# Lightning attention with a highway layer on one core: plain f32 loads with casts on Pool, and the feed-forward computed transposed in groups of four chunks

## The chip, the cores and the metric

The kernel runs on one core of a Trainium2 chip. The metric is device time in microseconds (us) for one execution; lower is better. TensorE is called PE, VectorE DVE, ScalarE ACT, GpSimd POOL (Pool), SyncE SP. Pool issues software DMAs, which can change the type on the way; SP and ACT issue hardware DMAs, which copy as is. PSUM is the memory that PE writes, SBUF the memory that DMA writes.

## What is computed

q, k and v have 4 batches, 8 heads, 768 positions and 64 features, all in f32. Positions go in blocks, and a state carries what came before:

```python
intra = einsum(qb, kb) * Dmask;  intra = einsum(intra, vb)   # Dmask = lam**(i-j) for i >= j
inter = einsum(qb * lam_pow, kv_state)
out   = intra + inter
kv_state = lam_block * kv_state + einsum(kb * rev_pow, vb)
# the heads side by side: x has 3072 rows and 512 columns
H = maximum(x @ w_h, 0);  T = sigmoid(x @ w_t + b_t)
y = T * H + (1 - T) * x                                      # 3072 x 512, f32
```

The kernels take blocks of 128 positions, which is the same sum cut otherwise, and put the powers of lam into v (pow_k) and into the attention's output (pow_q), so that the state itself needs no decay.

## The kernel before, in words

A chunk n is 128 positions of one batch with all 8 heads; there are 6 chunks a batch and N = 24 in all. The order of the work is written out by hand: the program calls helpers, and each engine runs its instructions in the order of these calls.

- Loads. k (one DMA per chunk, L58) and q (one per head, L53) are issued by Pool and cast to bf16 on the way. v comes as f32 on SP's queue (L64 for a whole batch, L67 for chunks of batch 0). The weights wh, wt are cast loads on Pool (L98, L99). The lam loads stand first on SP's queue (L71 to L75). Two buffers per batch tile (`load`), so a batch's loads are issued when the batch two before it ends (L262 to L266).
- `scale_v` (L165, Pool) multiplies a chunk of v by pow_k into bf16 vs. `trans_k` (L158 on PE, L160 on ACT) turns k, `trans_q` (L150, L151) turns a pair of heads of q for a whole batch, in the four turns before it is used. Both go through the one PSUM tile tr.
- `scores` (L173) makes s_ps from kT and qT, and DVE masks it (L176). `attn` adds the state's part (inter, L184) and the masked part (intra, L188) in o_ps; DVE multiplies by pow_q into xT (L191), features on partitions. `state` (L200) adds to kv_ps, and ACT copies it into s_bd (L204).
- The feed-forward of one chunk: `ffn_xh` turns xT back by matmuls with the identity (L209, copied by ACT to x_sb, L211) and computes x @ w_h with xT as the weights and wh moving (L214); DVE makes hmx = max(h, 0) - x (L216). `ffn_t` does x @ w_t (L221), adds the bias by one more matmul (L222: a row of ones times the bias, split in two bf16 rows prepared on DVE at L126 to L134), and ACT takes the sigmoid (L224). `combine` multiplies on DVE (thmx, L228), adds x on Pool (o_sb, L230), and SP stores (L231).
- A turn i of the loop (L245) runs ffn_xh(i-1), scores(i+1), scale_v(i+1), attn(i), state(i), trans_q, ffn_t(i-1), combine(i-1), trans_k(i+2). All PSUM tiles have one buffer.

Of the kernel before, what the change touches and what calls it, by code (L numbers as in the profile page):

```python
# [16 lines left out]
def kernel(  # L17
# [21 lines left out]
    N = B * NCH  # L39

# [7 lines left out]
    qb, kb, vf = {}, {}, {}  # L48

    def load_q(b):  # L50
        qb[b] = load.tile([QP, J, H, D], BF16, tag="qb", name=f"qb{b}")
        for h in range(H):
            nc.gpsimd.dma_start(out=qb[b][:, :, h, :], in_=q[b, h].rearrange("(p j) d -> p j d", j=J))  # L53

    def load_k(b, c):
        if b not in kb:
            kb[b] = load.tile([C, NCH, H, D], BF16, tag="kb", name=f"kb{b}")
        nc.gpsimd.dma_start(out=kb[b][:, c], in_=k[b, :, c * C:(c + 1) * C, :].rearrange("h p d -> p h d"))  # L58

    def load_v(b, cs=None):  # L60
        if b not in vf:
            vf[b] = load.tile([C, H, NCH, D], F32, tag="vf", name=f"vf{b}")
        if cs is None:
            nc.sync.dma_start(out=vf[b].rearrange("p h c d -> p (h c) d"),  # L64
                              in_=v[b].rearrange("h (c p) d -> p (h c) d", p=C))
        else:
            nc.sync.dma_start(out=vf[b][:, :, cs, :],  # L67
                              in_=v[b, :, cs * C:(cs + 1) * C, :].rearrange("h p d -> p h d"))

    lam_bc = singles.tile([128, H], F32)  # L70
    nc.sync.dma_start(out=lam_bc, in_=lam.partition_broadcast(128))  # L71
    lam_hp = singles.tile([128, NP], F32)
    lam_v = lam.rearrange("(p two) -> two p", two=2)
    nc.sync.dma_start(out=lam_hp[0:64, :], in_=lam_v[0].partition_broadcast(64))
    nc.sync.dma_start(out=lam_hp[64:128, :], in_=lam_v[1].partition_broadcast(64))  # L75
    load_k(0, 0)
    load_q(0)
    load_v(0, 0)
    load_v(0, 1)
    bt_f = singles.tile([128, DM], F32)  # L80
    nc.sync.dma_start(out=bt_f[0:1, :], in_=moe_b_t.partition_broadcast(1))
    nc.sync.dma_start(out=bt_f[32:33, :], in_=moe_b_t.partition_broadcast(1))
# [15 lines left out]
    nc.gpsimd.dma_start(out=wh, in_=moe_w_h.rearrange("(kc p) n -> p kc n", p=128))  # L98
    nc.gpsimd.dma_start(out=wt, in_=moe_w_t.rearrange("(kc p) n -> p kc n", p=128))  # L99
    for c in range(2, NCH):  # L100
        load_k(0, c)
        load_v(0, c)
    load_q(1)
    for c in range(NCH):
        load_k(1, c)
    load_v(1)
# [8 lines left out]
    nc.vector.tensor_copy(tq_f, tq_i)  # L115
    pk_ln = singles.tile([128, H, NCH], F32)
# [8 lines left out]
    ones_r = singles.tile([128, 128], BF16)  # L125
    nc.vector.memset(ones_r, 0.0)  # L126
    nc.vector.memset(ones_r[0:1, :], 1.0)
    nc.vector.memset(ones_r[32:33, :], 1.0)
    bt = singles.tile([128, DM], BF16)
    nc.vector.memset(bt, 0.0)  # L130
    bt_h = singles.tile([128, DM], BF16)
    nc.vector.tensor_copy(bt[0:1, :], bt_f[0:1, :])
    nc.vector.tensor_copy(bt_h[32:33, :], bt_f[32:33, :])
    nc.vector.tensor_tensor(bt[32:33, :], in0=bt_f[32:33, :], in1=bt_h[32:33, :], op=ALU.subtract)  # L134

    s_bd = []
    for i in range(2):
        t = singles.tile([128, NP, 128], BF16, name=f"s_bd{i}")
        nc.vector.memset(t, 0.0)
        s_bd.append(t)  # L140


    qT, kT, vs, masked, xT, x_sb, hps, tps, t_sb, hmx, kv_ps, o_ps = ({} for _ in range(12))

    def trans_q(b, hp):
        if hp == 0:
            qT[b] = load.tile([128, NP, NCH, J * PP], BF16, tag="qT", name=f"qT{b}")
        tr = ps.tile([128, J, QP], BF16, tag="tr", name="tr")
        for j in range(J):
            nc.tensor.transpose(tr[:, j, :], qb[b][:, j, 2 * hp:2 * hp + 2, :], id128[0:QP, 0:QP])  # L150
        nc.scalar.activation(qT[b][:, hp].rearrange("p c (q j) -> p (c q) j", j=J),  # L151
                             tr.rearrange("p j q -> p q j"), AF.Copy)

    def trans_k(n):
        b, c = divmod(n, NCH)
        tr = ps.tile([128, NP, C], BF16, tag="tr", name="tr")
        for hp in range(NP):
            nc.tensor.transpose(tr[:, hp, :], kb[b][:, c, 2 * hp:2 * hp + 2, :], id128)  # L158
        kT[n] = work.tile([128, NP, C], BF16, tag="kT", name="kT")
        nc.scalar.activation(kT[n], tr, AF.Copy)  # L160

    def scale_v(n):
        b, c = divmod(n, NCH)
        vs[n] = work.tile([C, H, D], BF16, tag="vs", name="vs", bufs=3)
        nc.gpsimd.tensor_tensor(vs[n], in0=vf[b][:, :, c, :], in1=pow_k[:, :, c, :].to_broadcast([C, H, D]), op=ALU.mult)  # L165
# [13 lines left out]
    def attn(n):  # L179
        b, c = divmod(n, NCH)  # L180
        o_ps[n] = ps.tile([128, NP, C], F32, tag="o", name="o_ps")
        for hp in range(NP):
            if c > 0:
                nc.tensor.matmul(o_ps[n][:, hp, :], lhsT=s_bd[n % 2][:, hp, :], rhs=qT[b][:, hp, c, :],  # L184
                                 start=(hp == 0), stop=False, skip_group_check=True)
        for hp in range(NP):
            for e in range(2):
                nc.tensor.matmul(o_ps[n][64 * e:64 * e + 64, hp, :], lhsT=vs[n][:, 2 * hp + e, :], rhs=masked[n][:, e, hp, :],  # L188
                                 start=(hp == 0 and c == 0), stop=True, skip_group_check=True)
        xT[n] = work.tile([128, NP, C], BF16, tag="xT", name="xT")  # L190
        nc.vector.tensor_tensor(xT[n], in0=o_ps[n], in1=pow_q[:, :, c * C:(c + 1) * C], op=ALU.mult)  # L191

    def state(n):
# [5 lines left out]
        for hp in range(NP):  # L199
            nc.tensor.matmul(kv_ps[b][:, hp, :], lhsT=kb[b][:, c, 2 * hp:2 * hp + 2, :], rhs=vs[n][:, 2 * hp:2 * hp + 2, :],  # L200
                             start=(c == 0 and hp == 0), stop=True, skip_group_check=True)
# [4 lines left out]
    def ffn_xh(n):  # L206
        x_ps = ps.tile([C, DM], F32, tag="x", name="x_ps")
        for kc in range(KC):
            nc.tensor.matmul(x_ps[:, kc * 128:(kc + 1) * 128], lhsT=xT[n][:, kc, :], rhs=id128, start=True, stop=True)  # L209
        x_sb[n] = work.tile([C, DM], BF16, tag="x_sb", name="x_sb", bufs=3)  # L210
        nc.scalar.activation(x_sb[n], x_ps, AF.Copy)  # L211
        h_ps = ps.tile([C, DM], F32, tag="h", name="h_ps")
        for kc in range(KC):
            nc.tensor.matmul(h_ps, lhsT=xT[n][:, kc, :], rhs=wh[:, kc, :], start=(kc == 0), stop=(kc == KC - 1))  # L214
        hmx[n] = work.tile([C, DM], BF16, tag="hmx", name="hmx")
        nc.vector.scalar_tensor_tensor(hmx[n], in0=h_ps, scalar=0.0, in1=x_sb[n], op0=ALU.max, op1=ALU.subtract)  # L216

    def ffn_t(n):
        t_ps = ps.tile([C, DM], F32, tag="t", name="t_ps")
        for kc in range(KC):  # L220
            nc.tensor.matmul(t_ps, lhsT=xT[n][:, kc, :], rhs=wt[:, kc, :], start=(kc == 0), stop=False)  # L221
        nc.tensor.matmul(t_ps, lhsT=ones_r, rhs=bt, start=False, stop=True)  # L222
        t_sb[n] = work.tile([C, DM], BF16, tag="t_sb", name="t_sb")
        nc.scalar.activation(t_sb[n], t_ps, AF.Sigmoid)  # L224

    def combine(n):
        thmx = work.tile([C, DM], BF16, tag="thmx", name="thmx")
        D_ENG.tensor_tensor(thmx, in0=t_sb[n], in1=hmx[n], op=ALU.mult)  # L228
        o_sb = work.tile([C, DM], F32, tag="o_sb", name="o_sb", bufs=3)
        nc.gpsimd.tensor_tensor(o_sb, in0=thmx, in1=x_sb[n], op=ALU.add)  # L230
        nc.sync.dma_start(out=out[n * C:(n + 1) * C, :], in_=o_sb)  # L231

    D_ENG = nc.vector

    scale_v(0)
    trans_k(0)
    for hp in range(NP):
        trans_q(0, hp)
    scores(0)
    for hp in range(NP):  # L240
        nc.scalar.activation(pow_q[:, hp, C:], tq_f[:, C:], AF.Exp, scale=ln_hp[:, hp:hp + 1])
    trans_k(1)

# [53 lines left out]
```

## Time and profile before

| | us |
|---|---|
| median of 3 runs | 197.85 (196.64 to 197.92) |
| the profiled execution, its own time | 197.84 |
| its span, first to last instruction | 196.0 |
| PE busy in the span | 105.8 |
| Pool busy | 101.8 |
| ACT busy | 74.7 |
| DVE busy | 74.3 |

The mean granted PE clock was 0.912 of full. HBM gave 20.98 MB and took 6.29 MB.

How to read the rows shown further on. A row of groups has line, engine, operation, output <- inputs, shapes, count, then busy us, mean ns of one, and the idle time before these instructions with what ended most of it. A row of the timeline has the start in us, the length, engine, line, operation, shapes and count. A row of waits has who waited for whom, the total in us, how often, and the longest. A row of windows has the stretch in us, its length, each engine's busy time with its instructions in brackets, the granted PE clock, the mean number of busy queue shares of the DMA engines, and GB/s written. Ends of matmuls are modelled, so starts are the safer reading.

### The profile page before, as it was taken

What the parts mean: (1) busy time and instruction counts of PE and PEld (TensorE: products, weight loads), DVE (VectorE), ACT (ScalarE), POOL (GpSimd) and SP (SyncE); (2) the same over time, 40 slices, a digit from 0 to 9 for tenths busy, and PEclk for the clock granted to TensorE, in tenths of its full rate; (3) what the DMA queues carried; (4) which work ended last, traced back from release to release, by engine and by line L of the source; (5) the groups of instructions that cost most, each with busy time, mean ns of one, the idle gap of its engine ahead of it and who ended that gap; (6) DMA issues with size and microseconds to landing.
All of it is one profiled execution on the core that took longest, in us unless ns stands there. A gap on an engine that the chain in (4) does not pass through costs nothing.

```text
span 196.0 us, 2858 instructions
## 1 busy us (share of the span) xinstructions
PE 105.8 (54%) x1080; PEld 61.0 (31%) x1080; DVE 74.3 (38%) x132; ACT 74.7 (38%) x142; POOL 101.8 (52%) x116
## 2 busy tenths in 40 slices
PE   0013420000797999000499999100299999999980
PEld 0012310000454555000255554000155555455440
DVE  0044040000155667300046666400036666677640
ACT  3045450000557663100147764100047765556630
POOL 7585531189304456943644445961835444655442
PEclk9999999999999999955589999955579999999999
DMA  0899999999501111999931111799962211112112
GB/s 5 69 170 171 187 182 228 185 129 141 37 0 53 55 55 57 182 209 159 140 64 54 57 53 53 142 214 168 141 34 80 82 55 53 57 55 110 53 53 107
DMA packets 66160, 20.10 MB, mean 103 GB/s; under 512 B 57442, under 2 KB 63074, under 8 KB 66148
## 3 DMA queue, kind: packets, MB, share of 16 engines
q0 software_dynamic: 51104, 7.34, 59.7%
q1 hardware_dynamic: 15044, 12.60, 26.0%
q8 instruction: 8, 0.13, 0.3%
q14 instruction: 4, 0.03, 0.1%
HBM read 20.98 MB, written 6.29 MB: 139 GB/s over the span
## 4 chain that ended last, share of the span: by engine, by line
issue 41%; DMA 30%; POOL 27%; POOLq 1%
DMA kb<-in_k_dram 24%; POOL vs L165 13%; DMA qb<-in_q_dram 6%; POOL qb L53 6%; POOL o_sb L230 4%; POOL kb L58 4%; POOLq L292 1%; POOLq L165 0%; POOLq L230 0%; POOLq L58 0%; POOLq L281 0%
## 5 line engine op out<-in xcount | busy, mean ns | idle before, releaser
L230 POOL TENSOR_TENSOR o_sb<-thmx,x_sb 128x512 f32<-128x512 bf16 x24 | 27.7, 1153 | 57.9 <-DVE thmx L228 57.9
L53 POOL DMA_DIRECT2D qb<-in_q_dram x32 | 24.7, 775 | 29.2 <-DMA kb<-in_k_dram 21.9
L176 DVE TENSOR_TENSOR masked<-s_ps,tri 128x512 bf16<-128x512 f32 x48 | 30.7, 681 | 9.7 <-PE s_ps L173 9.7
L204 ACT ACTIVATE s_bd<-kv_ps 64x256 bf16<-64x256 f32 x40 | 15.1, 378 | 49.8 <-PE kv_ps L200 49.4
L150 PE MATMUL tr<-id,qb 96*128 96x96 bf16 x128 | 10.2, 237 | 42.9 <-DMA qb<-in_q_dram 38.6
L228 DVE TENSOR_TENSOR thmx<-t_sb,hmx 128x512 bf16<-128x512 bf16 x24 | 10.2, 425 | 56.9 <-issue 51.2
L151 ACT ACTIVATE qT<-tr 128x768 bf16<-128x768 bf16 x16 | 13.0, 811 | 40.5 <-PE tr L150 40.3
L221 PE MATMUL t_ps<-wt,xT 128*128 128x512 bf16 x96 | 26.5, 400 | 0.0
L214 PE MATMUL h_ps<-wh,xT 128*128 128x512 bf16 x96 | 25.7, 392 | 0.0
L165 POOL TENSOR_TENSOR vs<-vf,pow_k 128x512 bf16<-128x512 f32 x24 | 25.4, 1068 | 0.0
L191 DVE TENSOR_TENSOR xT<-o_ps,pow_q 128x512 bf16<-128x512 f32 x24 | 16.4, 682 | 20.1 <-PE o_ps L188 20.1
L58 POOL DMA_DIRECT2D kb<-in_k_dram x24 | 21.7, 926 | 3.3 <-DMA qb<-in_q_dram 2.5
L216 DVE SCALAR_TENSOR_TENSOR hmx<-h_ps,x_sb 128x512 bf16<-128x512 f32 x24 | 16.6, 692 | 17.9 <-ACT x_sb L211 9.3
L150 PEld LDWEIGHTS <-qb 96*128 96x128 bf16 x128 | 8.2, 115 | 43.8 <-DMA qb<-in_q_dram 37.8
L188 PE MATMUL o_ps<-masked,vs 128*64 128x128 bf16 x192 | 10.3, 231 | 20.7 <-POOL vs L165 20.7
L224 ACT ACTIVATE t_sb<-t_ps 128x512 bf16<-128x512 f32 x24 | 14.3, 595 | 14.0 <-PE t_ps L222 14.0
L158 PE MATMUL tr<-id,kb 128*128 128x128 bf16 x96 | 10.3, 236 | 16.3 <-POOL id masks.py:199 11.8
L158 PEld LDWEIGHTS <-kb 128*128 128x128 bf16 x96 | 8.0, 106 | 23.6 <-DMA kb<-in_k_dram 10.9
L160 ACT ACTIVATE kT<-tr 128x512 bf16<-128x512 bf16 x24 | 14.2, 592 | 1.1 <-PE tr L158 0.7
L211 ACT ACTIVATE x_sb<-x_ps 128x512 bf16<-128x512 f32 x24 | 14.3, 597 | 0.1
L188 PEld LDWEIGHTS <-vs 128*64 128x64 bf16 x192 | 6.3, 113 | 23.4 <-POOL vs L165 21.0
L173 PE MATMUL s_ps<-qT,kT 64*128 64x128 bf16 x192 | 10.4, 229 | 3.3 <-ACT kT L160 2.9
(42 smaller groups left out, 94.0 us busy)
## 6 DMA issues: line engine op xcount, KB each, us to landing
out_dram<-o_sb SPq DMA_DIRECT2D x24, 256.0 KB, 2.0
kb<-in_k_dram POOLq DMA_DIRECT2D x24, 128.0 KB, 12.0
qb<-in_q_dram POOLq DMA_DIRECT2D x32, 96.0 KB, 10.5
vf<-in_v_dram SPq DMA_DIRECT2D x6, 256.0 KB, 10.8
wh<-in_moe_w_h_dram POOLq DMA_DIRECT2D x1, 512.0 KB, 14.0
wt<-in_moe_w_t_dram POOLq DMA_DIRECT2D x1, 512.0 KB, 17.1
vf<-in_v_dram SPq DMA_DIRECT2D x3, 0.2 KB, 12.2
lam_hp<-in_lam_dram SPq DMA_DIRECT2D x2, 1.0 KB, 7.4
```

Source lines behind the costliest of these rows:

```text
L53: nc.gpsimd.dma_start(out=qb[b][:, :, h, :], in_=q[b, h].rearrange("(p j) d -> p j d", j=J))
L58: nc.gpsimd.dma_start(out=kb[b][:, c], in_=k[b, :, c * C:(c + 1) * C, :].rearrange("h p d -> p h d"))
L150: nc.tensor.transpose(tr[:, j, :], qb[b][:, j, 2 * hp:2 * hp + 2, :], id128[0:QP, 0:QP])
L158: nc.tensor.transpose(tr[:, hp, :], kb[b][:, c, 2 * hp:2 * hp + 2, :], id128)
L165: nc.gpsimd.tensor_tensor(vs[n], in0=vf[b][:, :, c, :], in1=pow_k[:, :, c, :].to_broadcast([C, H, D]), op=ALU.mult)
L176: nc.vector.tensor_tensor(masked[n][:, e], in0=s_ps[:, e], in1=tri.to_broadcast([C, NP, C]), op=ALU.mult)
L188: nc.tensor.matmul(o_ps[n][64 * e:64 * e + 64, hp, :], lhsT=vs[n][:, 2 * hp + e, :], rhs=masked[n][:, e, hp, :], start=(hp == 0 and c == 0 ...
L191: nc.vector.tensor_tensor(xT[n], in0=o_ps[n], in1=pow_q[:, :, c * C:(c + 1) * C], op=ALU.mult)
L214: nc.tensor.matmul(h_ps, lhsT=xT[n][:, kc, :], rhs=wh[:, kc, :], start=(kc == 0), stop=(kc == KC - 1))
L216: nc.vector.scalar_tensor_tensor(hmx[n], in0=h_ps, scalar=0.0, in1=x_sb[n], op0=ALU.max, op1=ALU.subtract)
L221: nc.tensor.matmul(t_ps, lhsT=xT[n][:, kc, :], rhs=wt[:, kc, :], start=(kc == 0), stop=False)
L230: nc.gpsimd.tensor_tensor(o_sb, in0=thmx, in1=x_sb[n], op=ALU.add)
```

## The change

Loads: q, k and v are all plain f32 loads on SP's queue. Batch 0 comes in chunks (k, q, v of chunk 0, then of 1 and 2, later 3 to 5); the later batches come whole, one DMA each for q, k and v, issued at the end of turn 3 of the batch two before. The lam loads move to ACT's queue. The weights stay cast loads on Pool, and are issued after chunk 1's casts.

Casts: Pool casts k per chunk (`cast_k`, three chunks ahead), batch 0's q per chunk (`cast_q0`) and a later batch's q per pair of heads (`cast_q`). Chunk 0's two casts are DVE's. Batch 0's q is turned chunk by chunk (`trans_q0`).

Feed-forward: xT holds a group of four chunks (512 positions). A unit (g, j) computes 128 output features for the group, transposed: weights wh and wt stand still, xT moves. The bias is then one value per partition and goes into the sigmoid. hmx and thmx are made transposed too. `ffn_out` turns a chunk back: for each of four feature blocks, PE adds xT and thmx into one PSUM tile by matmuls with the identity, ACT copies it to f32 (DVE copies some of the last), and SP stores it. A turn runs one unit and one output; after the 24 chunks, eight more turns finish the last group.

```diff
+    def load_q(b):
+        qf[b] = load.tile([QP, H, J * D], F32, tag="qf", name=f"qf{b}")
+        nc.sync.dma_start(out=qf[b], in_=q[b].rearrange("h (p j) d -> p h (j d)", j=J))
+    def load_q0(c):
+        q0f[c] = load.tile([C, H, D], F32, tag="q0f", name=f"q0f{c}", bufs=3)
+        nc.sync.dma_start(out=q0f[c], in_=q[0, :, c * C:(c + 1) * C, :].rearrange("h p d -> p h d"))
...
+    def cast_k(n, eng=None):
+        kb[n] = work.tile([C, H, D], BF16, tag="kb", name="kb", bufs=4)
+        (eng or nc.gpsimd).tensor_copy(kb[n], kf[b][:, :, c, :])
+    def cast_q0(c, eng=None):
+        qb[c] = work.tile([C, H, D], BF16, tag="q0b", name="q0b")
+        (eng or nc.gpsimd).tensor_copy(qb[c], q0f[c])
+    def cast_q(b, hp):
+        qb[b, hp] = work.tile([QP, J, 2, D], BF16, tag="qb", name="qb")
+        nc.gpsimd.tensor_copy(qb[b, hp].rearrange("p j e d -> p e j d"),
+                              qf[b][:, 2 * hp:2 * hp + 2, :].rearrange("p e (j d) -> p e j d", j=J))
...
+    def ffn_h(g, j):
+        for kc in range(KC):
+            nc.tensor.matmul(h_ps, lhsT=wh[:, kc, j * 128:(j + 1) * 128], rhs=xT[g][:, kc, :],
+                             start=(kc == 0), stop=(kc == KC - 1))
+        nc.vector.scalar_tensor_tensor(hmx[g, j], in0=h_ps, scalar=0.0, in1=xT[g][:, j, :], op0=ALU.max, op1=ALU.subtract)
+    def ffn_t(g, j):
...
+        nc.scalar.activation(t_sb, t_ps, AF.Sigmoid, bias=bt_col[:, j:j + 1])
+        nc.vector.tensor_tensor(thmx[g][:, j, :], in0=t_sb, in1=hmx[g, j], op=ALU.mult)
+    def ffn_out(n, eng="act"):
+        for j in range(NP):
+            for i, t in enumerate((xT[g], thmx[g])):
+                nc.tensor.matmul(x_ps[:, j * 128:(j + 1) * 128], lhsT=t[:, j, r * C:(r + 1) * C], rhs=id128,
+                                 start=(j == 0 and i == 0), stop=(i == 1), skip_group_check=True)
+        o_sb = work.tile([C, DM], F32, tag="o_sb", name="o_sb", bufs=4)
...
+    cast_k(0, nc.vector)
+    cast_q0(0, nc.vector)
     scale_v(0)
     trans_k(0)
+    trans_q0(0)
     scores(0)
+    for c in range(3, NCH):
+        load_kv(0, "k", k, c)
+        load_q0(c)
+        load_kv(0, "v", v, c)
+    load_q(1)
+    load_kv(1, "k", k)
+    load_kv(1, "v", v)
+    cast_k(1)
+    cast_q0(1)
+    scale_v(1)
...
+    nc.gpsimd.dma_start(out=wh, in_=moe_w_h.rearrange("(kc p) n -> p kc n", p=128))
+    nc.gpsimd.dma_start(out=wt, in_=moe_w_t.rearrange("(kc p) n -> p kc n", p=128))
+    cast_k(2)
+    scale_v(2)
+    cast_q0(2)
+    while i < N or units or outs:
+        if i + 3 < N:
+            cast_k(i + 3)
+            scale_v(i + 3)
+        if i + 3 < NCH:
+            cast_q0(i + 3)
+        if c < NP and b + 1 < B:
+            cast_q(b + 1, c)
+        if i + 2 < N:
+            trans_k(i + 2)
+        if i < N:
+            inter(i)
+        if i + 1 < N:
+            scores(i + 1)
+        if i < N:
+            intra(i)
+            state(i)
+        if i + 2 < NCH:
+            trans_q0(i + 2)
+        if 1 <= c <= NP and b + 1 < B:
+            trans_q(b + 1, c - 1)
+        unit = units.pop(0) if units else None
+        if unit:
+            ffn_h(*unit)
+        if outs:
+            ffn_out(outs.pop(0), "dve" if i >= N and i % 2 else "act")
+        if unit:
+            ffn_t(*unit)
+            if unit[1] == NP - 1:
+                outs += range(unit[0] * G, unit[0] * G + G)
+        if i < N and i % G == G - 1:
+            units += [(i // G, j) for j in range(NP)]
+        if c == 3 and b + 2 < B:
+            load_q(b + 2)
+            load_kv(b + 2, "k", k)
+            load_kv(b + 2, "v", v)
+        i += 1
```

More of the change, by code (lines that the diff above doesn't have):

```diff
@@ L60, in load_v @@
[L60 to L68, printed above, removed]
+    kf, vf, qf, q0f = {}, {}, {}, {}
```

180 lines of the change are left out of this document (77 added, 103 removed).

## The prediction, made before the result was known

> **What bounds the kernel now.** I read the page's slices and queues first, then the list of waits, then the timeline of one fed chunk.
>
> ```profile
> PE   0013420000797999000499999100299999999980
> DMA  0899999999501111999931111799962211112112
> ...
> q0 software_dynamic: 51104, 7.34, 59.7%
> ```
>
> Each digit is a slice of 4.9 us. PE is at nine tenths in three stretches and stands still before each of them, and there the DMA row is at nine. Inside the stretches DMA is nearly idle. So loads and matmuls take turns. The queue that fills the engines is the software one: q and k, cast on their way, 59.7% of all engine time for 7.34 MB.
>
> ```profile
> PE tr L150 <- DMA qb<-in_q_dram: 38.6, 4, 17.7
> POOL qb L53 <- DMA kb<-in_k_dram: 21.9, 10, 5.5
> ...
> 48.67 0.40 PEld L188 LDWEIGHTS <-vs 128*64 128x64 bf16 x8 [20.96 <-POOL vs L165]
> ```
>
> PE lost 38.6 us to q in four waits. It got its first scaled v at 48.67 us, because Pool issues all those DMAs in order ahead of its multiply. In a fed stretch the period is PE's own:
>
> ```profile
> 169.66 0.40 PE L209 MATMUL x_ps<-id,xT 128*128 128x128 bf16 x4 [0.34 <-DVE xT L191]
> 169.89 1.03 PE L214 MATMUL h_ps<-wh,xT 128*128 128x512 bf16 x4
> 170.85 0.40 PE L173 MATMUL s_ps<-qT,kT 64*128 64x128 bf16 x8
> 171.18 0.40 PE L184 MATMUL o_ps<-qT,s_bd 128*128 128x128 bf16 x4
> 171.51 0.41 PE L188 MATMUL o_ps<-masked,vs 128*64 128x128 bf16 x8
> 171.86 0.40 PE L200 MATMUL kv_ps<-vs,kb 128*128 128x128 bf16 x4
> 172.09 1.03 PE L221 MATMUL t_ps<-wt,xT 128*128 128x512 bf16 x4
> 172.95 0.38 PE L222 MATMUL t_ps<-bt,ones_r 128*128 128x512 bf16 x1
> 173.17 0.39 PE L158 MATMUL tr<-id,kb 128*128 128x128 bf16 x4
> 173.57 0.23 PE L209 MATMUL x_ps<-id,xT 128*128 128x128 bf16 x1
> ...
> 151.19 0.51 PE L150 MATMUL tr<-id,qb 96*128 96x96 bf16 x8
> 151.53 0.38 PE L221 MATMUL t_ps<-wt,xT 128*128 128x512 bf16 x1
> ```
>
> One chunk takes 173.57 - 169.66 = 3.91 us. From start to start (which leaves out the modelled ends): x 0.23, four wide matmuls 0.86, scores 0.33, inter 0.33, intra 0.35, state 0.23, bias 0.22, transposes 0.21. That sums to 3.62; the rest waits for DVE and ACT. A chunk with q transposes adds 0.34.
>
> **PE after the change.** The bias matmul goes (-0.22), the turn-back has eight narrow matmuls for four (+0.23), the wide ones stay eight a chunk: 1.45 attention + 1.72 + 0.46 = 3.63, and 3.97 with q. The wait for xT goes, since the feed-forward reads a group finished earlier. I allow 0.10 and 0.15 for handoffs: 3.73 and 4.12.
>
> **The other engines** must fit under that.
>
> ```profile
> L176 DVE TENSOR_TENSOR masked<-s_ps,tri 128x512 bf16<-128x512 f32 x48 | 30.7, 681 | 9.7 <-PE s_ps L173 9.7
> L191 DVE TENSOR_TENSOR xT<-o_ps,pow_q 128x512 bf16<-128x512 f32 x24 | 16.4, 682 | 20.1 <-PE o_ps L188 20.1
> L216 DVE SCALAR_TENSOR_TENSOR hmx<-h_ps,x_sb 128x512 bf16<-128x512 f32 x24 | 16.6, 692 | 17.9 <-ACT x_sb L211 9.3 <-PE h_ps L214 8.5
> L228 DVE TENSOR_TENSOR thmx<-t_sb,hmx 128x512 bf16<-128x512 bf16 x24 | 10.2, 425 | 56.9 <-issue 51.2
> L204 ACT ACTIVATE s_bd<-kv_ps 64x256 bf16<-64x256 f32 x40 | 15.1, 378 | 49.8 <-PE kv_ps L200 49.4
> L151 ACT ACTIVATE qT<-tr 128x768 bf16<-128x768 bf16 x16 | 13.0, 811 | 40.5 <-PE tr L150 40.3
> L160 ACT ACTIVATE kT<-tr 128x512 bf16<-128x512 bf16 x24 | 14.2, 592 | 1.1 <-PE tr L158 0.7
> L211 ACT ACTIVATE x_sb<-x_ps 128x512 bf16<-128x512 f32 x24 | 14.3, 597 | 0.1
> L224 ACT ACTIVATE t_sb<-t_ps 128x512 bf16<-128x512 f32 x24 | 14.3, 595 | 14.0 <-PE t_ps L222 14.0
> L165 POOL TENSOR_TENSOR vs<-vf,pow_k 128x512 bf16<-128x512 f32 x24 | 25.4, 1068 | 0.0
> L94 POOL IOTA tq_i<- 128x768 int32 x1 | 0.8, 768 | 0.0
> ```
>
> DVE: 2 x 0.681 + 0.682 + 0.692 + 0.425 = 3.16 a chunk, as before. ACT: 0.592 + 2 x 0.378 + 0.811 + 0.597 + 0.595 = 3.35 with q (the output copy takes the place of x_sb). Both lie beside PE's 4.12. Pool loses its DMA issues and the add, and gains casts that no row shows. The bounds for 128x512 are 0.51 (the iota's 1.0 ns an element, one stream) and 1.07 (the multiply, which reads vf with the same strides and more). I take 0.8, and 1.5 for a q cast of twice the elements. Pool then needs 0.8 + 1.07 + 1.5 = 3.4 with q, 1.9 without. The GPSIMD Engine Reference of the Trainium skill (section Engine selection) calls one-input work on Pool roughly line rate; by it the cast is about 0.43 (an estimate at its 1.2 GHz), and the sum below falls by only 0.7, since v gates that place.
>
> The small edits I cost at nothing. The bias's set-up on DVE (L126 to L134) goes, and the memsets move up: both lie in the first 17 us, beside loads that end later. Batch 0's q is turned in four transposes and one 128x512 copy a chunk (0.21 on PE, about 0.59 on ACT, by k's rows) for a quarter of the old qT copies: PE and ACT wait for loads and casts there anyway. The bias column's load has until turn 4 to arrive. If that cover were gone, all of it together would cost under 5 us.
>
> **The loads.** All of q, k, v is now plain f32 on SP's queue. Two bounds for 256-byte pieces, and the price of long rows from the stores (256 KB each):
>
> ```profile
> 10.00:20.00 10.00, 2.63 (x27) 2.25 (x28) 4.13 (x12) 5.00 (x10) 7.18 (x13) 1.00 1.79 171
> 126.00:128.00 2.00, 0.00 (x0) 0.00 (x0) 0.00 (x0) 0.00 (x0) 2.00 (x3) 0.82 1.33 249
> 156.00:158.00 2.00, 1.66 (x18) 0.90 (x15) 1.20 (x3) 1.93 (x4) 0.32 (x1) 1.00 0.35 131
> ...
> out_dram<-o_sb SPq DMA_DIRECT2D x24, 256.0 KB, 2.0
> ```
>
> The last three columns are clock, DMA share and GB/s; in the first row software casts run too, and count at half of what they read. At 171 to 249 GB/s a batch of k or of v (1.57 MB) takes 6.3 to 9.2 us; I take 7.5, the middle. A store keeps the engines busy 0.35 x 2 = 0.70 us, so q of a later batch, in 2 KB rows, takes 4.2. A batch's loads and six stores are then 19.2 + 4.2 = 23.4 us, against 4 x 4.12 + 2 x 3.73 = 23.9 of PE: hidden, barely. Each load is issued six chunks early, and SP blocked behind it delays stores by less than their four buffers.
>
> **The start, where the gain is cut.** Pool, in order, decides it.
>
> ```profile
> 10.49 0.20 ACT L111 ACTIVATE ln_hp<-lam_hp 128x4 f32<-128x4 f32 x1 [6.97 <-DMA lam_hp<-in_lam_dram]
> 10.71 1.28 ACT L120 ACT_TABLE_LOAD   x1
> ...
> 13.85 0.24 ACT L120 ACTIVATE pow_k<-pk_ln 128x48 f32<-128x48 f32 x1 [1.85 <-DVE pk_ln L117]
> 14.17 0.78 POOL L98 DMA_DIRECT2D wh<-in_moe_w_h_dram  x1
> ...
> 52.37 1.91 PE L214 MATMUL h_ps<-wh,xT 128*128 128x512 bf16 x4
> ```
>
> The lam loads move to ACT's queue at about the same time: landing 10.5, then 0.20, the table load 1.28 and 0.24 give pow_k at 12.3 (it need not wait for DVE's pk_ln as it did, since Pool's iotas now run first). Pool then runs three multiplies, four casts (k and q of chunks 1 and 2) and two weight issues (2 x 0.78, say 1.5): 3.2 + 3.2 + 1.5, done at 20.2. The q0 buffer for chunk 5 has to wait for that last cast (three buffers), and SP is in order, so chunk 5's q and v and all of batch 1 queue behind it. With 2.0 to start (issue, then the store's 2.0 less its 0.7), 2.5 for two chunk pieces and 4.2 for q, batch 1's q lands at 28.9, k at 36.4, v at 43.9.
>
> The loop's first turn has Pool cast a quarter of batch 1's q. That cast waits until 28.9, and the casts of chunks 4 and 5 stand behind it: 30.4, then 4.2 a turn (two casts, multiply, q cast), 34.6, 38.8. In turn 3 the multiply of chunk 6 waits for v, 43.9; it ends at 45.0 and the q cast at 46.5. In turn 4 PE waits for that cast, transposes (0.34, handoff 0.1) and does the first feed-forward unit, 1.72 and 0.9 more for a clock that is still low (four matmuls took 1.91 at 52.37 and 1.03 later; half of that loss). Turn 5 starts at 49.6.
>
> **Sum.** Turns 5 to 23: 11 x 3.73 + 8 x 4.12 - 3 x 0.46 (no outputs yet) = 72.6, to 122.2. Four units of the last group with outputs: 4 x 2.18 = 8.7, to 130.9. Sigmoid, product, handoffs: 1.3. Four outputs on one PSUM buffer: 4 x (0.46 + 0.60 + 0.2) = 5.0, to 137.2.
>
> ```profile
> 192.96 0.33 SPq L231 DMA_DIRECT2D out_dram<-o_sb  x1
> ```
>
> This last store landed 2.0 later, near 195.0, and the span ends at 196.0: 2.1 (with a handoff) and 1.0 more give a span of 140.3. The profiled run took 197.84 with a span of 196.0, so 1.84 lies outside; its time is the median's 197.85. Forecast: **142 us**.
>
> **Rivals.**
> A, the loads become the bound. For it: the margin above is 0.5 us a batch by the middle price, and at 171 GB/s a batch is 4.2 + 18.4 + 4.2 = 26.8, over PE's 23.9. Against it: the 249 row held with other traffic beside it. Price: the start +4.0 (0.6 for the two pieces, 3.4 for k and v), two batches +2.9 each: 152.
>
> B, DVE and Pool get in each other's way. The product thmx is DVE's one instruction with both inputs in SBUF. Until now it ran while Pool waited for it (57.9 us at L230), so the trace has no overlap; masked, with one SBUF input, kept 681 ns beside Pool. If thmx waits for a running Pool instruction, up to 1.5 us, DVE needs 4.7 a chunk: 4.7 less the loop's mean of 3.9, 19 times: +15, 157.
>
> ```profile
> POOL o_sb L230 <- DVE thmx L228: 57.9, 24, 9.6
> ```
>
> The Trainium skill's page SBUF — State Buffer (Who interferes with whom) says exactly this of two SBUF inputs beside a reading GpSimd; no row here shows it. The wait is free up to about 0.7 us, since thmx stands behind the sigmoid anyway.
>
> C, slower than before: the casts are much dearer than the multiply. With x for a 128x512 cast, Pool's chain above puts turn 5 at about 32 + 17x once Pool and not v gates it. Turns 5 to 20 hold 16 k casts, 16 multiplies and 8 double q casts, 32x + 17. Then come about 13 for the last three and a half turns, and the 18.1 of the tail and 1.8: 82 + 49x. At x = 2.6 that is 209. It ties with before at x = 2.36, over twice the multiply of the same tile for less work, and no row speaks for that.
>
> D, the gaps stay: PE still waits for a load at batches 2 and 3, because issue from SP comes late. At the old 18 us each, 178. Against it: the buffers are free when the issue comes, and nothing on Pool holds it.
>
> **Chances.** Forecast 0.70, A 0.13, B 0.11, D 0.03, C 0.03. The low end is both cheap ends (249 GB/s, casts at 0.51, no handoffs, full clock), 5 + 2.3 + 0.9 below, rounded out to 131; the high end takes in A and B: 157. About 1% is what a measurement of this kernel can tell (three runs spread 0.65%). Faster 0.96, same 0.01 (D with longer gaps), slower 0.03.
>
> **What would show it.** Right: no PE stall over 3 us after turn 5; clock 1.00 through one long dense stretch; first wide matmul near 47 us; a period of 3.7 to 4.1; Pool's casts between 0.5 and 1.1 us; a wait of Pool for batch 1's q ending near 29. Wrong: PE slices at zero in the middle (A or D), thmx starting late with the sigmoid done (B), Pool at nine tenths in the loop (C).

## The result, and the profile after

The kernel after takes **161.46 us** (median of 4 runs, 160.52 to 162.11) against 197.88 for the kernel before in the same session (196.64 to 199.29): a ratio of 0.8154, with a 95% interval of 0.8083 to 0.8225. The direction was right. The size was not: 142 was forecast, and 161.46 lies above the range of 131 to 157. The profiled run took 161.08 with a span of 159.3. The time outside the span is thus about what was added for it, and the miss is inside: 159.3 - 140.3 = 19.0 us.

The slices (now 3.98 us each) and the queues of the page:

```profile
PE   0104661100275689999999989309999999999740
PEclk9999999999999999999999999955799999999985
DMA  4299999999999999999579999971111212313333
...
q1 hardware_dynamic: 33840, 25.17, 72.2%
q0 software_dynamic: 1056, 1.05, 3.9%
```

Before, loads and matmuls took turns and PE stood still three times. Now DMA works from 8 us on with one short break, and PE lies beside it from 57 us. But the DMA row falls to ones only at 107 us, and up to there PE shows a late start, a stop in slices 26 and 27, and a low clock after that. Cut at these places (busy times of the engines, then clock, DMA share, GB/s):

```profile
8.00:30.00 22.00, 8.44 (x80) 5.66 (x79) 5.06 (x8) 11.71 (x23) 9.29 (x12) 1.00 1.23 209
30.00:42.00 12.00, 0.00 (x0) 0.00 (x0) 0.00 (x0) 0.00 (x0) 0.35 (x1) 1.00 1.15 218
42.00:57.00 15.00, 9.31 (x96) 7.45 (x96) 3.77 (x6) 6.42 (x12) 7.77 (x11) 1.00 1.09 213
57.00:76.00 19.00, 18.62 (x199) 11.45 (x202) 13.97 (x24) 12.50 (x22) 13.30 (x16) 1.00 1.11 220
76.00:80.00 4.00, 3.95 (x55) 2.75 (x54) 2.82 (x5) 3.32 (x7) 1.71 (x2) 1.00 0.42 107
80.00:105.00 25.00, 20.06 (x260) 13.44 (x261) 14.78 (x25) 13.67 (x25) 12.40 (x15) 0.96 1.04 222
105.00:112.00 7.00, 4.23 (x23) 2.50 (x24) 3.61 (x5) 3.70 (x7) 4.41 (x5) 0.50 0.31 115
```

The last column is the finding: 209, 218, 213, 220 and 222 GB/s while DMA is at work, whatever is being read (256-byte pieces, q in 2 KB rows, weights). One stream of reads fills the time from 8 to 105 us, with one hole at 76 to 80. That the forms agree so well is partly chance: further down, two of them prove slow for separate reasons.

Who waits for it, in the timelines of Pool, ACT and PE:

```profile
19.61 0.60 POOL L136 CAST q0b<-q0f 128x512 bf16<-128x512 f32 x1
...
41.65 1.04 POOL L148 CAST qb<-qf 96x1024 bf16<-96x1024 f32 x1 [13.04 <-DMA qf<-in_q_dram]
56.70 1.06 POOL L132 TENSOR_TENSOR vs<-vf,pow_k 128x512 bf16<-128x512 f32 x1 [7.23 <-DMA vf<-in_v_dram]
59.84 1.49 PE L214 MATMUL h_ps<-xT,wh 128*128 128x512 bf16 x3 [0.22 <-issue]
62.42 0.39 PE L163 MATMUL tr<-id,kb 128*128 128x128 bf16 x4
...
105.21 1.06 POOL L132 TENSOR_TENSOR vs<-vf,pow_k 128x512 bf16<-128x512 f32 x1 [6.24 <-DMA vf<-in_v_dram]
105.83 0.60 ACT L239 ACTIVATE o_sb<-x_ps 128x512 f32<-128x512 f32 x1 [7.13 <-DMA out_dram<-o_sb]
107.54 0.80 PE L156 MATMUL tr<-id,qb 96*128 96x96 bf16 x8 [6.59 <-ACT kT L165]
```

Pool's cast of chunk 2's q, which frees the buffer for chunk 5's q, ends at 20.21, as forecast (20.2). But batch 1's q is cast at 41.65 (28.9 was forecast), the first wide matmul runs at 59.84 (47), turn 5 starts at 62.42 (49.6). Near 105 two waits end together: Pool's for batch 3's v, and ACT's for a free output buffer. PE stands 6.59 us behind the second, since ACT's kT copy stands behind ACT's output copy.

SP's issues show both causes. The second column is how long SP stood in an issue, or in several neighbours of one kind, counted at the end of the row:

```profile
4.41 5.09 SPq L70 DMA_DIRECT2D q0f<-in_q_dram  x1
...
17.88 4.19 SPq L61 DMA_DIRECT2D kf<-in_k_dram  x1
22.17 3.40 SPq L70 DMA_DIRECT2D q0f<-in_q_dram  x1
...
27.83 1.05 SPq L70 DMA_DIRECT2D q0f<-in_q_dram  x1
...
30.28 1.15 SPq L66 DMA_DIRECT2D qf<-in_q_dram  x1
...
75.78 4.34 SPq L242 DMA_DIRECT2D out_dram<-o_sb  x2
80.22 0.38 SPq L66 DMA_DIRECT2D qf<-in_q_dram  x1
81.98 13.64 SPq L58 DMA_DIRECT2D vf<-in_v_dram  x1
95.72 11.06 SPq L242 DMA_DIRECT2D out_dram<-o_sb  x5
```

An issue takes about 1 us while the engines are saturated. Three took 5.09, 4.19 and 3.40. So SP reached chunk 5's q only at 27.83, when its buffer had been free since 20.21. Further down, batch 3's loads stand behind the store of turn 9 (80.22; the hole in the stream), and the next store stands behind those loads, until 95.72.

The parts that held, by the groups and one fed turn:

```profile
L127 POOL CAST kb<-kf 128x512 bf16<-128x512 f32 x23 | 14.0, 609 | 7.1 <-PE kv_ps L205 6.9
L148 POOL CAST qb<-qf 96x1024 bf16<-96x1024 f32 x12 | 12.7, 1059 | 18.4 <-DMA qf<-in_q_dram 18.4
...
87.16 0.39 PE L163 MATMUL tr<-id,kb 128*128 128x128 bf16 x4
...
90.55 0.39 PE L163 MATMUL tr<-id,kb 128*128 128x128 bf16 x4
...
72.06 0.69 ACT L225 ACTIVATE t_sb<-t_ps,bt_col 128x512 bf16<-128x512 f32 x1 [0.46 <-PE h_ps L214]
76.02 0.69 ACT L225 ACTIVATE t_sb<-t_ps,bt_col 128x512 bf16<-128x512 f32 x1 [0.27 <-PE t_ps L222]
```

A turn without q takes 90.55 - 87.16 = 3.39 us, one with q 76.02 - 72.06 = 3.96 (3.73 and 4.12 forecast).

### The profile page after: what moved, and what is told of

The parts are those of the page before. It is cut to its first block, busy times and chain, and to the rows that moved or that the text cites. A ratio compares the mean times of both kernels' runs of the same rounds, so it can differ in the third digit from the quotient of the medians.

```text
span 159.3 us, 2882 instructions
## 1 busy us (share of the span) xinstructions
PE 105.4 (66%) x1127; PEld 69.3 (44%) x1144; DVE 75.5 (47%) x131; ACT 77.2 (48%) x140; POOL 57.1 (36%) x76
## 4 chain that ended last, share of the span: by engine, by line
PE 45%; issue 18%; DMA 16%; POOL 7%; SPq 5%; ACT 5%; DVE 1%; POOLq 0%; ACTq 0%
PE h_ps L214 11%; PE t_ps L222 10%; DMA qf<-in_q_dram 7%; PE x_ps L235 6%; DMA out_dram<-o_sb 6%; PE o_ps L191 4%; SPq L70 4%; PE s_ps L173 3%; PE tr L156 3%; DMA vf<-in_v_dram 3%; PE kv_ps L205 3%; PE tr L163 3%; PE o_ps L184 2%; POOL vs L132 2%; POOL qb L148 2%
## 5 line engine op out<-in xcount | busy, mean ns | idle before, releaser
L132 POOL TENSOR_TENSOR vs<-vf,pow_k 128x512 bf16<-128x512 f32 x24 | 25.8, 1077 | 43.4 <-DMA vf<-in_v_dram 25.4
L214 PE MATMUL h_ps<-xT,wh 128*128 128x512 bf16 x87 | 25.4, 397 | 0.8 <-issue 0.4
L222 PE MATMUL t_ps<-xT,wt 128*128 128x512 bf16 x88 | 24.9, 396 | 0.3
L225 ACT ACTIVATE t_sb<-t_ps,bt_col 128x512 bf16<-128x512 f32 x24 | 16.5, 687 | 12.1 <-PE t_ps L222 10.2
L239 ACT ACTIVATE o_sb<-x_ps 128x512 f32<-128x512 f32 x20 | 11.9, 597 | 20.6 <-PE x_ps L235 13.5
L148 POOL CAST qb<-qf 96x1024 bf16<-96x1024 f32 x12 | 12.7, 1059 | 18.4 <-DMA qf<-in_q_dram 18.4
L217 DVE SCALAR_TENSOR_TENSOR hmx<-h_ps,xT 128x512 bf16<-128x512 f32 x24 | 16.4, 682 | 2.3 <-PE h_ps L214 2.2
L127 POOL CAST kb<-kf 128x512 bf16<-128x512 f32 x23 | 14.0, 609 | 7.1 <-PE kv_ps L205 6.9
L235 PE MATMUL x_ps<-id,xT 128*128 128x128 bf16 x96 | 14.0, 226 | 2.7 <-ACT o_sb L239 1.4
L235 PE MATMUL x_ps<-id,thmx 128*128 128x128 bf16 x96 | 14.3, 227 | 0.4 <-DVE thmx L228 0.4
L235 PEld LDWEIGHTS <-thmx 128*128 128x128 bf16 x96 | 9.7, 101 | 6.4 <-issue 3.4
```

The costliest lines, as they stand in the source:

```text
L148: nc.gpsimd.tensor_copy(qb[b, hp].rearrange("p j e d -> p e j d"), qf[b][:, 2 * hp:2 * hp + 2, :].rearrange("p e (j d) -> p e j d", j=J))
L214: nc.tensor.matmul(h_ps, lhsT=wh[:, kc, j * 128:(j + 1) * 128], rhs=xT[g][:, kc, :], start=(kc == 0), stop=(kc == KC - 1))
L217: nc.vector.scalar_tensor_tensor(hmx[g, j], in0=h_ps, scalar=0.0, in1=xT[g][:, j, :], op0=ALU.max, op1=ALU.subtract)
L222: nc.tensor.matmul(t_ps, lhsT=wt[:, kc, j * 128:(j + 1) * 128], rhs=xT[g][:, kc, :], start=(kc == 0), stop=(kc == KC - 1))
L225: nc.scalar.activation(t_sb, t_ps, AF.Sigmoid, bias=bt_col[:, j:j + 1])
L235: nc.tensor.matmul(x_ps[:, j * 128:(j + 1) * 128], lhsT=t[:, j, r * C:(r + 1) * C], rhs=id128, start=(j == 0 and i == 0), stop=(i == 1), s ...
```

## The experiments

From the two profiles I had two causes in mind: the reads (their rate, and what stands ahead of batch 1's q) delay the start, and SP's one queue or batch 3's late v makes the stop at 101 to 107 us. Letters name theories within the text that introduces them; Q is SP's one queue for all loads and stores. In each run a time is a median, and the kernel after is 161.46. The runs fall into five sessions, in which the kernel before took 197.52 to 199.46; a difference of one or two us between runs of different sessions is therefore no difference. Two numbers split the span of a profiled run: the start of the first hmx (L217; 61.4 in the kernel after), and the rest of the span behind it (159.3 - 61.4 = 97.9).

**Which half brings the gain.** e6 has the new loads, casts and attention with the old feed-forward; e8 the old loads with the new feed-forward, in the old order of a turn.

```
e6:  for i in range(N + 1):  ...  ffn_xh(i - 1) ... ffn_t(i - 1); combine(i - 1)   # loads, casts of after
e8:  while i < N or units or outs:  ...  ffn_h(*unit); ffn_out(...); ffn_t(*unit)  # load_q/k/v of before
```

> Half of the change alone: the plain loads, Pool's casts and the attention as in the kernel after, with the feed-forward of the kernel before, one chunk at a time, its bias matmul and Pool's add of the output. Where does the gain of 36 us come from? If from the loads (as the prediction's start and gaps have it), this kernel takes 160 to 175: the same start near 57, PE's period 4.0 to 4.3, Pool's add of 1.15 us beside 0.61 + 1.08 + 1.06 of casts and multiply still under it, a shorter tail than the kernel after (no last group to finish). If the feed-forward brings most of it, 180 to 195. Pool's add waits in order for the product of its chunk and would hold the casts back: then above 175 with Pool's wait for thmx large.

> The other half alone: the feed-forward for groups of four chunks, turned back by PE, with the loads of the kernel before (casts on the way in Pool's software queue). If the loads set the time before, this kernel stays within 190 to 200, since PE stands for the same loads; Pool without its add issues its loads earlier, which may give up to 10 us: 186 to 198 in all. If the feed-forward brings most of the gain, 165 to 180.

e6 took 171.44 (ratio 0.8624, 0.8572 to 0.8676). e8's four runs took 193.45 to 198.45, beside 199.46 (197.53 to 199.81) before: between 1 and 6 us less, and these runs can't say how much. So the loads alone bring 28 us, the feed-forward alone a few at most, and on top of the loads it brings 10. A cheaper turn need not be what brings them: in e6 Pool stood 20.6 us in two waits for an output buffer, behind stores that stand behind loads on SP's queue, and the kernel after has one such wait, of 7.13. How the 10 us divide was not tried. While PE stands for loads, a cheaper turn is worth little; that is also why a reader of before's profile should cost the loads first.

**The start: lam.** e1 takes the logarithm for head pairs from the broadcast tile, so the two loads of lam in 4-byte pieces on ACT's queue go.

```
-    nc.scalar.dma_start(out=lam_hp[0:64, :], in_=lam_v[0].partition_broadcast(64))
-    nc.scalar.dma_start(out=lam_hp[64:128, :], in_=lam_v[1].partition_broadcast(64))
-    nc.scalar.activation(ln_hp, lam_hp, AF.Ln)
+    nc.scalar.activation(ln_hp[r, :], lam_v[r, e, :], AF.Ln)      # two halves, from lam_bc
```

> The two lam loads with 4-byte pieces go; ln_hp is taken from lam_bc, which is loaded anyway. Theory Q (one hardware queue reads at about 217 GB/s whatever the row length, so that the last load's landing near 105 us, and what follows it, set the end): SP's third-chunk issue no longer stands for 5.09 us at 4.41, all later loads land 4 to 5 us earlier, and the time falls by 4 to 5 us, to about 157. Rival P (Pool's order of casts at the start sets the end, as the prediction had it): pow_k is ready about 5 us earlier too, but Pool is then waiting for v anyway, and the time falls by under 2 us.

156.82, the 4.6 us less that Q expected. SP's fifth issue, 5.09 us long, is now

```profile
4.55 1.09 SPq L70 DMA_DIRECT2D q0f<-in_q_dram  x1
```

batch 1's q is cast at 37.49, 4.2 earlier, and hmx starts at 56.6, 4.8 earlier. Two loads of 1 KB held up megabytes.

**The start: weights.** e13 leaves the weights' loads out (`memset(wh, 0.0)`, `memset(wt, 0.0)`).

> Leaves out the loads of the two weights (both are zeros instead), so the feed-forward computes with zeros. Theory B (the start is bytes through the DMA engines: 4.7 MB of batch 0 and 2.1 MB of weights stand ahead of batch 1's q, at 220 to 310 GB/s): SP's two issues of 4.19 and 3.40 us at 17.88 and 22.17 fall to about 1.2 each, batch 1's q lands 5 us earlier, near 36.5, and the time falls from 161.5 to 155.5 to 157.5. Theory K (Pool's chain of casts and multiplies gates the issue of the last pieces, as the prediction had it): the issues keep their times and so does the kernel, 160 to 162.

155.86. The issues of 4.19 and 3.40 us and Pool's first q cast become

```profile
17.76 1.32 SPq L61 DMA_DIRECT2D kf<-in_k_dram  x1
19.18 1.09 SPq L70 DMA_DIRECT2D q0f<-in_q_dram  x1
...
36.19 1.04 POOL L148 CAST qb<-qf 96x1024 bf16<-96x1024 f32 x1 [12.68 <-DMA qf<-in_q_dram]
```

Batch 1's q is there 5.5 us earlier and hmx starts at 56.6. Theory B holds, K falls: bytes held the last pieces of batch 0 back, not Pool's casts (which had freed the buffer 7.6 us before SP came to use it).

**What sets the read rate.** e3 and e7 only load, one transfer after another.

> Loads alone, nothing is computed: stages of 1.57 MB, one after the other, each waited for. On SP's queue q in 2 KB rows, k in 256-byte rows, k in 12 KB rows; then 2 KB rows on SP and ACT at once, 256-byte rows on SP and ACT at once, 2 KB rows on SP and Pool at once, 256-byte rows on Pool alone; last one store of 6.3 MB. Theory Q: 7 to 8 us a stage on SP alone for all three row lengths (215 to 225 GB/s), and 290 GB/s or more with two queues. Rival R (the chip's reads end at about 220 GB/s): two queues give no more than one, 14 us for the two. Rival S (pieces): 12 KB rows take under 5 us, 256-byte rows over 8. The store goes at over 350 GB/s by all.

> Computes nothing of the reference: loads alone, one after another, 1.57 MB each, from SP's queue. In order: 12 KB of contiguous source to a partition; the same source order cut into 2 KB pieces by gaps in the tile; into 256-byte pieces; 2 KB rows of which neighbours go to neighbouring partitions; 16 KB to each of 96 partitions; q head by head; q as the kernel loads it; the store at the end. Theory L (the length of a piece decides): the first and the fifth at 400 GB/s or more, near 6.5 us from one to the next; all others at 200 to 270, near 9 to 10. Theory X (the order of addresses in memory decides): the second and the third as fast as the first, and only the last two q forms slow. Theory P (96 instead of 128 partitions): the fifth slow too, at three quarters of the first.

In e3, 1.57 MB from SP alone took 9.7 us in q's rows and 9.4 in k's 256-byte pieces, but 6.2 as 12 KB a partition. Two queues moved twice the bytes, 3.15 MB, in 15.5 to 16.9 us, that is 186 to 203 GB/s with the time to start and land, no more than the 209 to 222 of the one queue in the kernel: Q's reason, the one queue, is not what limits reading. The store moved 384 GB/s. In e7 the DVE copy behind each transfer tells when it has landed:

```profile
34.14 0.22 DVE L53 COPY tb<-ta 128x48 f32<-128x48 f32 x1 [7.16 <-DMA ta<-in_k_dram]
...
41.64 0.22 DVE L53 COPY tb<-ta 128x48 f32<-128x48 f32 x1 [7.03 <-DMA ta<-in_k_dram]
...
51.83 0.22 DVE L53 COPY tb<-ta 128x48 f32<-128x48 f32 x1 [9.71 <-DMA ta<-in_k_dram]
...
59.20 0.22 DVE L53 COPY tb<-ta 128x48 f32<-128x48 f32 x1 [6.89 <-DMA ta<-in_v_dram]
...
68.83 0.22 DVE L53 COPY tb<-ta 128x48 f32<-128x48 f32 x1 [9.16 <-DMA ta<-in_v_dram]
...
87.65 0.22 DVE L53 COPY tb<-ta 128x48 f32<-128x48 f32 x1 [9.36 <-DMA ta<-in_q_dram]
```

The waits in brackets: 12 KB to a partition 7.16; the same in 2 KB pieces 7.03; in 256-byte pieces 9.71; 2 KB rows over 128 partitions 6.89; 16 KB to each of 96 partitions 9.16; q head by head 8.51; q as the kernel loads it 9.36. Each form was taken once, and 12 KB to a partition had taken 6.26 in e3, so differences under 1 us say nothing. Two separate things are slow: pieces of 256 bytes, and 96 partitions even in rows of 16 KB (P; L holds for 256 bytes only, X falls). The Trainium skill's page SBUF — State Buffer, in its section on the DMA port swizzle, says that partitions 0 to 63 reach half of the SBUF's 16 DMA ports and the upper half the rest; 96 partitions would then load half the ports fully and half of them half, which by an estimate from that map is three quarters of the full rate. 7.16 / 9.16 = 0.78 is close to it; that the ports are the reason is not shown by it.

**q in 128 partitions.** e9 changes one constant and what hangs on it.

```
-    J = 8
+    J = 6
```

> One size changed: six positions of q to a partition instead of eight, so that q of batches 1 to 3 lands in 128 partitions in rows of 1.5 KB instead of in 96 in rows of 2 KB; the turning takes six 128x128 transposes instead of eight 96x96, and Pool's cast 768 elements a partition instead of 1024. Theory P (96 partitions halve the rate: 16 KB to each of 96 partitions took 9.13 us where 12 KB to each of 128 took 7.14): q of a batch takes 4.7 to 5.2 us instead of 7.2, batch 1's q lands near 39 instead of 41.65, Pool's cast falls from 1.06 to about 0.8, and the time from 161.5 to 157 to 159.5. Theory L (rows of 2 KB or less are slow whatever they land in): q takes 7 us as before, and the time stays within 160.3 to 162.5.

156.21, a larger gain than forecast. It comes at both ends: hmx starts 2.9 us earlier, and the rest behind it is 2.7 shorter, where q of batches 2 and 3 comes. From issue to landing (us min/median/max), first e9, then the kernel after:

```profile
DMA to landing us min/median/max: 7.6/8.0/15.3
```
```profile
DMA to landing us min/median/max: 11.3/11.3/18.0
```

Batch 1's q is cast at 38.52 (3.1 earlier), hmx starts at 58.5, and the cast itself falls from 1059 to 825 ns.

**The stop at 101 to 107 us.** Three tries.

```
e2:  load_kv(b, ...) whole    ->  for ch in range(NCH): load_kv(b, "k", k, ch); load_kv(b, "v", v, ch)
e4:  kf, vf bufs 2 -> 3;  if c == 3 and b + 2 < B  ->  if c == 0 and b + 2 < B
e5:  nc.sync.dma_start(out=out[...], in_=o_sb)  ->  nc.scalar.dma_start(out=out[...], in_=o_sb)
```

> k and v of batches 1 to 3 come in chunks (256-byte pieces), k and v of a chunk in turn, instead of whole batches. Theory Q: bytes and not pieces set the pace, so the last load still lands near 105 us, but chunk 18's k and v land some 11 us earlier, the PE gap at 101 to 108 us shrinks to under 2 us with the low clock behind it, and the time falls by 6 to 10 us, to 151 to 155. Rival S (short pieces are the cost, as the bounds 171 to 249 GB/s had it): the loads get slower, a batch takes over 25 us, and the time rises or stays within 2 us.

> k and v of a batch get three buffers, and the loads of the batch two ahead are issued at the end of its turn 0 in place of turn 3. Theory Q: the loads stand in one queue, so they only close SP's idle time from 68.6 to 80.2 us, in which the DMA engines had work until about 76 and then little; the last load lands 4 to 5 us earlier, stores queue behind loads and cost some of it back: 157 to 161. Rival D (the late issue is what leaves PE without data): the gap at 101 to 108 us goes whole, and the time falls by 8 us or more, to 153 or less.

> The only edit: each output is stored from ACT's queue, right behind the copy that makes it, instead of from SP's, where it stands behind batch 3's loads. Theory F (one in-order queue: the stores wait behind the loads, the output buffers run out, ACT stops): ACT's wait of 7.1 us for an output buffer at 105.8 us goes, and with it most of the stop of PE and the low clock after it. Pool's v for batch 3 then still comes late (its whole load, landing near 105), so PE still stops for about 2 to 4 us there. Expected 152 to 157 us, against 161.5. Theory V (v's own arrival sets the gap): v lands when it landed, so the time stays within 159 to 163. Against F would also speak a new wait of ACT for its own issue of stores.

e2: 160.94. The 6 to 10 us that Q expected did not come, although Pool now had v in time. (S forecast such a time, but not for this reason: the reads kept their rate.) ACT still waited for its output buffer:

```profile
105.16 0.60 ACT L239 ACTIVATE o_sb<-x_ps 128x512 f32<-128x512 f32 x1 [6.29 <-DMA out_dram<-o_sb]
```

So the stop stays when v is in time. e4: 164.88, slower, and outside both forecasts. With the loads earlier, all stores stand behind them; in SP's timeline the first are

```profile
91.42 8.40 SPq L242 DMA_DIRECT2D out_dram<-o_sb  x4
```

e5: 155.84. PE's and the clock's rows have no stop any more, and batch 3's loads are issued at 69.64 instead of 80.22:

```profile
PE   0103555100056847999999999999999999999460
PEclk9999999999999999999999999999999999999955
...
69.64 6.85 SPq L66 DMA_DIRECT2D qf<-in_q_dram  x1
...
102.61 1.06 POOL L132 TENSOR_TENSOR vs<-vf,pow_k 128x512 bf16<-128x512 f32 x1 [4.17 <-DMA vf<-in_v_dram]
```

The last row settles V: Pool still waits 4.17 us for batch 3's v, which comes only 2.6 us earlier than before, and PE does not stop (F had left 2 to 4 us for that). With v in time the stop stays (e2), with v late it goes (e5). Theory F holds, and it cuts both ways: loads waited for stores on SP's queue, and stores for loads. The rest behind the first hmx is 152.8 - 62.0 = 90.8, 7.1 less.

**An earlier use of the same stream.** e14 casts batch 1's q in turns 2 and 3 and turns it in turns 3 and 4; e15 adds e2's pieces.

```
-        if c < NP and b + 1 < B: cast_q(b + 1, c)
+        if b == 0 and c in (2, 3): cast_q(1, 2 * c - 4); cast_q(1, 2 * c - 3)
+        if b > 0 and c < NP and b + 1 < B: cast_q(b + 1, c)
```

> The kernel after with batch 1's q cast in turns 2 and 3 and turned in turns 3 and 4, nothing else. If PE's wait for q (13.5 us in turn 1) alone sets the start, turns 1 and 2 run beside the loads and the time falls by 5 to 8 us: 153.5 to 156.5. If v of batch 1 as one whole load (landing at 56.7) is late next, Pool's multiply of turn 3 waits for it ahead of the last q casts, and the first wide matmul comes near 60 as before: at most 2 us less, 159.5 to 161.5.

> The same with k and v of batches 1 to 3 in chunk pieces. Pieces alone gave 0.5 us. If the two waits cover one another (q in turn 1, v in turn 3), both edits together give what neither gives alone: 153 to 156.5 us, with the first wide matmul near 53. If each stands for itself, the sum of the two single effects, 158.5 to 161.

e14: 164.11, slower than both forecasts: v, late next, is waited for ahead of the last two q casts (hmx at 64.8). e15: 161.0, no gain, though hmx starts at 55.2, 6.2 earlier. The start was won and given back: PE then stood for batch 2's q,

```profile
66.60 1.03 POOL L148 CAST qb<-qf 96x1024 bf16<-96x1024 f32 x1 [7.87 <-DMA qf<-in_q_dram]
```

and the rest grew to 104.8. The stop is where it was: ACT waits 7.06 us for its output buffer, until 106.21. My expectation fell. Here the stream of reads on SP's queue, and the stores behind it, set the pace up to 105 us, and an order that only uses the stream earlier gains nothing.

**All together.** e10 joins e1, e5 and e9; e11 adds e15's two edits; e12 adds e4's to that.

> Three edits together: no 4-byte loads of lam on ACT's queue, outputs stored from ACT's queue, q in 128 partitions. If the three are separate costs at separate places they add up: 161.5 - 4.6 - 5.6 - 2.5 = 148.8, so 147 to 151. If the start is set by something else once q comes earlier (the turns 1 to 3 with their 5.9 us of handoffs between PE and ACT, or v of batch 1), the third gives nothing: 151 to 153.

> The three edits, and two more: k and v of batches 1 to 3 in chunk pieces, and batch 1's q cast in turns 2 and 3 and turned in turns 3 and 4, so that turns 0 to 2 need only batch 0's data. Theory W (the start is set by PE's wait for batch 1's q, 13.4 us in turn 1, as the prediction had it): turns 1 and 2 now run before that q lands, their handoffs of 5.9 us a turn lie beside the loads, and the start is then set by the pieces of batch 1: 5 to 9 us less than with the three edits, 140 to 144. Theory T (the loads as a whole set it: all of batch 1 must be read at about 220 GB/s by turn 4 or so): at most 2 us less, 146 to 149.

> The version before, and the loads of batches 2 and 3 issued three turns earlier, into third buffers of k and v. With the stores on ACT's queue nothing stands behind the loads on SP, so what cost 3.4 us in the kernel after cannot happen. If the loads of batch 3 still hold the turns 12 to 16 at 4.1 us instead of 3.5, this gives 2 to 4 us: 137 to 142. If PE is fed there anyway, nothing: within 1 us of the version before.

e10: 146.89. The single effects are 4.6, 5.6 and 5.3, which would give 146.0: they nearly add up. e11: **139.93** (ratio 0.7054, 0.701 to 0.7098), faster than both kernels. The order that gave nothing in the kernel after is worth 7.0 us once the stream is shorter and no store stands in it (which of its two edits brings them, and which of the two conditions it needs, was not tried apart). Its PE row is at nine tenths from slice 14 on, of 3.45 us each:

```profile
PE   0141870667266999999999999999999999999350
```

e12: 140.19, nothing more; PE is fed already.

| kernel | time | first hmx | rest of the span |
|---|---|---|---|
| after | 161.46 | 61.4 | 97.9 |
| e1, e13, e9 (shorter stream) | 156.82, 155.86, 156.21 | 56.6, 56.6, 58.5 | 97.0, 98.5, 95.2 |
| e5 (stores apart) | 155.84 | 62.0 | 90.8 |
| e15 (used earlier) | 161.0 | 55.2 | 104.8 |
| e10, e11 | 146.89, 139.93 | 54.3, 46.9 | 90.7, 91.2 |

## Why the prediction was wrong in size

The miss of 19.0 us has two parts: turn 5 starts 62.42 - 49.6 = 12.8 late, and the rest takes 159.3 - 62.42 = 96.9 where 90.7 were forecast, 6.2 more.

- **The loop and the tail** were right but for the stop, in part by luck. Without it (e5, from turn 5 at 63.43 to 152.8) they take 89.4. In that, turns 5 to 23 are 69.1 us where 72.6 were forecast, and the tail is 20.3 where 18.1 were: two errors that nearly cancel.
- **The casts** were over-sized (0.609 against 0.8, 1.059 against 1.5). It does not matter, for Pool waits for data, and C falls. The 0.43 that the prediction worked out from the Trainium skill's page GPSIMD Engine Reference (Engine selection) is too low: the measured 0.609 decides.
- **The start failed**, and by one term: batch 1's q landed at 41.65 instead of 28.9. From there to turn 5 took 20.8 us where 20.7 were forecast. The failing step is "the q0 buffer for chunk 5 has to wait for that last cast ... With 2.0 to start, 2.5 for two chunk pieces and 4.2 for q". It let Pool's chain set the last pieces and priced only these by the rate. Pool's cast ended on time, at 20.21, but nothing waited for it: SP came to chunk 5's q at 27.83, held back by the reads ahead. 4.7 MB of batch 0 stood there, and 2.1 MB of weights. My own 7.5 us a tensor would have put batch 0 alone at 3 x 7.5 = 22.5 us of reading. By experiments (start of q's cast, 41.65 in the kernel after): without lam's small loads 37.49, without the weights 36.19, with q in 128 partitions 38.52, that is 4.2, 5.5 and 3.1 earlier, together the 12.8. Each was taken away alone, so that the sum comes out so exactly is partly luck; e10, which has the first and the third, starts the cast at 34.62, 7.0 earlier.
- **q's price failed**: "q of a later batch, in 2 KB rows, takes 4.2", from the stores' rate. Stores write from 128 partitions; q goes to 96. In the stream q costs 1.57 MB / 218 GB/s = 7.2. A batch with its stores is then 7.2 + 2 x 7.2 + 4.2 = 25.8 us, over the 4 x 3.96 + 2 x 3.39 = 22.6 of PE: not "hidden, barely" but longer. (In e5 PE still does not stop for it.) k and v at 7.2 were right (7.5).
- **"SP blocked behind it delays stores by less than their four buffers"** failed. The stores waited from 81.98 to 95.72, nearly four turns, and then for the engines; ACT stood 7.13 us, PE 6.59, and the clock fell to 0.50 for 7 us. Cost: 5.6 us (e5). "Against it" in rival D, that the buffers are free when the issue comes, missed that SP itself was not free.
- **The rivals.** A, the loads as the bound, is what happened, at 0.13 and 152: its price kept q at 4.2 and the start at 4 more. D's gap came, once, at batch 3, and for SP's order. B is real but small: thmx took 484 ns on average against 425. Four of its 24 executions started while a Pool instruction ran, and these took 0.53, 0.54, 0.91 and 1.12 us; the other twenty took 0.42 or 0.43:

```profile
L228 DVE TENSOR_TENSOR thmx<-t_sb,hmx x24: 424/426/1121, 63.3 to 150.4; 128x512 bf16<-128x512 bf16 x24
```

The Trainium skill's page SBUF — State Buffer (Who interferes with whom), which the prediction cited for it, agrees as far as these four go.

- **What was right for another reason.** The 20.7 us from q to turn 5 counted Pool's wait for v. PE in fact had a chain of its own there, which ended at about the same time; that the two agree is luck. In e2, with v in pieces, Pool's last q cast of batch 1 starts at 50.60 instead of 57.71, and hmx still starts at 61.3: the chain alone sets it. Turns 1 to 3 hold no feed-forward, and k, q and the old q0 share one PSUM buffer for transposes, so each waits for ACT's copy of the one before:

```profile
48.68 0.80 PE L156 MATMUL tr<-id,qb 96*128 96x96 bf16 x8 [1.12 <-ACT qT L144]
50.38 0.59 PE L163 MATMUL tr<-id,kb 128*128 128x128 bf16 x4 [0.90 <-ACT qT L157]
...
54.59 0.80 PE L156 MATMUL tr<-id,qb 96*128 96x96 bf16 x8 [1.12 <-ACT qT L144]
```

54.59 - 48.68 = 5.91 us a turn, longer than a full turn of the loop. The matmuls are slower here (0.59 for a group that takes 0.39 later). The prediction put such a slowness at the first feed-forward unit down to a clock that is still low; the granted clock reads 1.00 in the row from 42 to 57 us, so the reason is not shown here. That the shared buffer makes the chain was read from these waits and not tried.

## What to carry to other kernels

Before costing a loop, add up every byte that the first and the last needed load have ahead of them, small parameters and weights included, at a rate measured for that shape and that number of partitions; where the stream is longer than the compute beside it, shortening the stream gains, and an earlier use of it alone can be given back whole. Look at each in-order queue for the loads that stand behind a store and the stores that stand behind a load. And try single edits in company: an order that is worth nothing while another bound holds was worth 7 us without it.

## What the hardware showed that was not expected

- A load of 1.57 MB into 96 partitions took 9.16 us, and as many bytes into 128 took 7.16, with rows of 12 KB and more.
- Pieces of 256 bytes took 9.71 us for 1.57 MB against 7.03 in pieces of 2 KB from the same source order. The Trainium skill's page DMA: Bandwidth & Descriptors (Specifications) puts the limit of the full rate at 512 bytes; 256 agrees, and nothing between was tried.
- A second queue added nothing to one that reads: 3.15 MB on two in 15.5 us or more, 203 GB/s at best, and 209 to 222 GB/s on one in the kernel.
- Two loads of 1 KB in 4-byte pieces on another queue held one issue of SP for 5.09 us instead of 1.09.
